# Attention with 16 queries per head: queries transposed on the DVE from eight strided loads, QK weights kept for two chunks, a finer cut of the second last V piece

## The chip, the cores and the metric

The kernel runs on one core of a Trainium2 chip. The metric is the device time of one execution in microseconds (us), the median of several. The record marks every one of them as fast, at a granted clock of 0.894 to 0.926, and each kernel was run beside the kernel before on the same chip.

Words used: PE is the matmul engine and PEld its weight loads, DVE the vector engine, ACT the scalar engine, SP the sync engine, which here does nothing but issue loads. DMA is the set of engines, 16 by the profile's page, that move data between the chip's main memory and the on-chip memory (SBUF). A DMA queue is called by the engine that issues on it. Partitions are the rows of a tile in SBUF: 128 in the 128x2048 of the DVE's lines below.

## The reference

```python
B, H, Sq, Skv, Dh = 8, 16, 16, 2048, 256          # bfloat16 throughout

def reference(q, k, v):
    scale = q.shape[-1] ** -0.5
    scores = jnp.einsum('bhqd,bhkd->bhqk', q, k) * scale
    attn = _softmax(scores, axis=-1)
    return jnp.einsum('bhqk,bhkd->bhqd', attn, v)
```

There are 128 heads. K and V are 134 MB each, q and the output 1 MB each. Every byte of K and V is used for only 16 queries, so the loads were expected to bound the time. In the profile of the kernel before, their queue accounts for 98.5% of the DMA engines.

## The kernel before

It treats eight heads as a group (16 groups) and K and V as 64 pieces of 2 MB each. For K piece `i`, SP loads `KN`; the DVE transposes it into `KB` in two halves, `kt(i,0)` and `kt(i,1)`; PE multiplies it with the query weights `QW` (`qk`). After four pieces the DVE takes the row maximum, ACT does the exponential, the DVE transposes the result (`pt`, `px`), and PE multiplies with V (`pv`). The queries reach `QW` through PE transposes (`qprep`) and a scaling copy on ACT (`qwb`).

```python
NT = 64; PT_TOK = 32; R_KN = 3; R_KB = 4; R_V = 5        # buffers: 3 K pieces, 4 K halves, 5 V pieces
qg = q.rearrange("b h s d -> (b h s) d").rearrange("(g p) d -> p g d", p=128)
# ... the order of the loads on SP: K0, q, K1, K2, K3, K4, V0, K5, V1, ...
        for i in range(NP):
            seq.append(("k", i))
            if i == 0:
                seq.append(("q", 0))
            if 4 <= i < NP - 3:
                seq.append(("v", i - 4))
# ...
        tail = {NP - 2: [32], NP - 1: [16, 8, 8]}        # tokens per load of the last two V pieces
        def k_load(i):                                   # a K buffer is free when kt of its old piece is done
            s = i % R_KN
            return J("sp", "ld", lambda eng: eng.dma_start(
                KN[:, s], ku[i // 2, :, PT_TOK * (i % 2):PT_TOK * (i % 2) + PT_TOK, :]),
                [("kt", i - R_KN, 1) if i >= R_KN else None], dma=(sem_kn[s], 16 * (i // R_KN + 1)))
# ...
                j_q = J("sp", "ld", lambda eng: eng.dma_start(QR[:], qg), dma=(sem_q, 16))
# ...
        def kt(i, h):                                    # a K half waits for the QK that used its buffer
                j_kt[i, h] = J("dve", "kt", lambda eng: emit_kt(eng, i, h),
                               [j_k[i], ("qk", i - R_KB // 2, h) if i >= R_KB // 2 else None])
        def qk(i):                                       # one job of 8 matmuls for each half
                for c in range(2):
                    j_qk[i, c] = J("pe", "qk", lambda eng, c=c: emit_qk(eng, i, c),
                                   [("kt", i, c), ("qwb", g), ("exp", g - 1, i % 2) if g and i % 4 < 2 else None])
# ... the order on the DVE
        kt(0, 0)
        kt(0, 1)
        for g in range(G):
            for r in (1, 2, 3):
                kt(4 * g + r, 0)
                kt(4 * g + r, 1)
            # max(g); kt(4g+4, 0); pt(g), px(g), small sums; kt(4g+4, 1); eviction of group g-1
```

The DVE works through its list in order: while it waits at one operation, the work behind it waits too. In this program SP issues K `i+3` only when `kt(i,1)` is done, and a V load behind a waiting K load waits with it (V0 goes out behind K4, at 21.5 us). And `kt(i+2)` cannot start before `qk(i)` has used the buffer.

Of the kernel before, what the change touches and what calls it, by code (L numbers as in the profile page):

```python
# [4 lines left out]
ACTF = mybir.ActivationFunctionType  # L5
ALU = mybir.AluOpType
AX = mybir.AxisListType
BF16 = mybir.dt.bfloat16
F32 = mybir.dt.float32
# [4 lines left out]
R_KB = 4  # L14
R_V = 5
# [10 lines left out]
def bass_standalone__softmax_full_bidir__sampling_kernel(  # L26
# [6 lines left out]
    B, H, SQ, D = q.shape  # L33
# [3 lines left out]
    G = NH // 8  # L37
    NP = 4 * G
    scale = float(D) ** -0.5
# [1 line left out]

    ku = k.rearrange("b h s d -> (b h s) d").rearrange("(u p t) d -> u p t d", p=128, t=NT)
    vu = v.rearrange("b h s d -> (b h s) d").rearrange("(u p t) d -> u p t d", p=128, t=NT)
    qg = q.rearrange("b h s d -> (b h s) d").rearrange("(g p) d -> p g d", p=128)

    with ExitStack() as es:
        ec = es.enter_context
        KN = ec(nc.sbuf_tensor("KN", [128, R_KN, PT_TOK, D], BF16))
        KB = ec(nc.sbuf_tensor("KB", [128, R_KB, PT_TOK // 2, D], BF16))
        VB = ec(nc.sbuf_tensor("VB", [128, R_V, PT_TOK, D], BF16))  # L50
        QR = ec(nc.sbuf_tensor("QR", [128, G, D], BF16))
        QW = ec(nc.sbuf_tensor("QW", [128, 2, 2, 8, 128], BF16))
        P_sb = ec(nc.sbuf_tensor("P_sb", [128, 2048], BF16))
        PC = ec(nc.sbuf_tensor("PC", [128, 2, NT // 2, 32], BF16))
# [10 lines left out]

        S_ps = ec(nc.psum_tensor("S_ps", [128, 4, 512], F32))
        O_ps = ec(nc.psum_tensor("O_ps", [128, 3, 512], F32))
        XP_ps = ec(nc.psum_tensor("XP_ps", [128, 8, 128], BF16))

        sem_kn = [ec(nc.semaphore("s_kn%d" % i)) for i in range(R_KN)]  # L70
        sem_v = [ec(nc.semaphore("s_v%d" % i)) for i in range(R_V)]
# [17 lines left out]

        block = ec(nc.Block())  # L90

        KNf = KN[:].bitcast(F32)
        KBf = KB[:].bitcast(F32)

        def ap_of(t_ap, offset, dims):
            return bass.AP(tensor=t_ap.tensor, offset=offset, ap=[list(t_ap.ap[0])] + [list(d) for d in dims])
# [8 lines left out]
            iv = ident[:]  # L105
            return eng.tensor_reduce(out=mask[:], in_=ap_of(iv, iv.offset, [[1, 2], [2, 64]]), axis=AX.X, op=ALU.add)

        def emit_qprep(eng, g):
            qv = QR[:, g, :]
            for bp in range(8):  # L110
                b, par = bp // 2, bp % 2
                for a in range(4):
                    ins = eng.transpose(XP_ps[32 * a:32 * a + 32, bp, :], ap_of(qv, qv.offset + 64 * b + par, [[2, 32]]),  # L113
                                        ident[:], tile_position=(0, 32 * a))
            return ins

        def emit_qwb(eng, g):
            for a in range(4):
                dv = QW[32 * a:32 * a + 32, g % 2, 0, 0, :]
                sv = XP_ps[32 * a:32 * a + 32, 0, :]  # L120
                ins = eng.activation(ap_of(dv, dv.offset + 32 * a, [[8 * 128 + 1, 2], [128, 8], [2, 16]]),  # L121
                                     ap_of(sv, sv.offset + 16 * a, [[64, 2], [128, 8], [1, 16]]),
                                     ACTF.Copy, scale=scale)
            return ins

        def emit_kt(eng, i, h):
# [1 line left out]
            return eng.transpose(KBf[:, (2 * i + h) % R_KB].rearrange("p t i -> p (t i)"),  # L128
                                 KNf[:, i % R_KN].rearrange("p t i -> p (t i)")[:, n * h:n * h + n])

        def emit_qk(eng, i, c):
            g, Gh, half = i // 4, (i % 4) // 2, i % 2
            kb0 = KB[:, (2 * i + c) % R_KB, 0, :]
            for bp in range(8):
                b, par = bp // 2, bp % 2
                ins = eng.matmul(S_ps[:, 2 * half + c, :], QW[:, g % 2, Gh, bp, :],  # L136
                                 ap_of(kb0, kb0.offset + 64 * b + par, [[D, 16], [2, 32]]),
                                 start=(Gh == 0 and bp == 0), stop=(Gh == 1 and bp == 7))
            return ins

        def emit_max(eng, g):
            return eng.tensor_reduce(out=negm[:, g:g + 1], in_=S_ps[:].rearrange("p c n -> p (c n)"),  # L142
                                     axis=AX.X, op=ALU.max, negate=True)
# [45 lines left out]
        for j in range(NP):  # L189
            g, r = j // 4, j % 4  # L190
            v_of.append((2 * g + r % 2, r // 2) if g < last - 1 else (2 * g + r // 2, r % 2))
        seq = []
        for i in range(NP):
            seq.append(("k", i))
            if i == 0:
                seq.append(("q", 0))
            if 4 <= i < NP - 3:
                seq.append(("v", i - 4))
            elif i == NP - 2:
                seq.append(("v", i - 5))  # L200
        seq += [("v", j) for j in range(NP - 6, NP)]

        j_k, j_v, j_kt, j_qk, j_pv = {}, {}, {}, {}, {}
        j_qwb, j_qprep, j_exp, j_pt, j_px, j_max, j_rab = {}, {}, {}, {}, {}, {}, {}
        j_ea, j_eb, j_st = {}, {}, {}
        tail = {NP - 2: [32], NP - 1: [16, 8, 8]}

        def k_load(i):
            s = i % R_KN
# [8 lines left out]
        def v_load(j, a, n, sem):  # L218
            u, h = v_of[j]
            if j < NP - 2:  # L220
                deps = [("pvuse", j - R_V)] if j >= R_V else []
            else:
                deps = [("kt", j - 1, 0), ("kt", j - 1, 1)]
            return J("sp", "ld", lambda eng: eng.dma_start(  # L224
                v_buf(j)[:, a:a + n, :], vu[u, :, PT_TOK * h + a:PT_TOK * h + a + n, :]), deps, dma=sem)

        for what, i in seq:
            if what == "k":
                j_k[i] = k_load(i)
            elif what == "q":  # L230
                j_q = J("sp", "ld", lambda eng: eng.dma_start(QR[:], qg), dma=(sem_q, 16))
            elif i < NP - 2:
                j_v[i] = [v_load(i, 0, PT_TOK, (sem_v[i % R_V], 16 * (i // R_V + 1)))]
            else:
                parts, a = [], 0
                for x, n in enumerate(tail[i]):
                    sem = ec(nc.semaphore("s_vt%d_%d" % (i, x)))
                    parts.append(v_load(i, a, n, (sem, 16)))
                    a += n
                j_v[i] = parts  # L240

        def qprep(g):
            if g < G:
                j_qprep[g] = J("pe", "qprep", lambda eng: emit_qprep(eng, g), [j_q, j_ident, ("qwb", g - 1) if g else None])

        def qwb(g):
            if g < G:
                j_qwb[g] = J("act", "qwb", lambda eng: emit_qwb(eng, g),
                             [("qprep", g), j_qwz, ("qk", 4 * g - 5, 1) if g >= 2 else None])

        def kt(i, h):
            if i < NP:
                j_kt[i, h] = J("dve", "kt", lambda eng: emit_kt(eng, i, h),
                               [j_k[i], ("qk", i - R_KB // 2, h) if i >= R_KB // 2 else None])

        def qk(i):
            if i < NP:
                g = i // 4
                for c in range(2):
                    j_qk[i, c] = J("pe", "qk", lambda eng, c=c: emit_qk(eng, i, c),  # L260
                                   [("kt", i, c), ("qwb", g), ("exp", g - 1, i % 2) if g and i % 4 < 2 else None])

        def pv(g, p):
            if g < 0:
# [47 lines left out]
                            dma=(sem_st[g % 2], 16 * (g // 2 + 1)))  # L312


        qprep(0)
        qprep(1)
        for g in range(G):
            if g < last:
                qk(4 * g)
                qk(4 * g + 1)  # L320
                pv(g - 1, 0)
                qk(4 * g + 2)
                qk(4 * g + 3)
                pv(g - 1, 1)
                qprep(g + 2)
            else:
                qk(4 * g)
                qk(4 * g + 1)
                pv_single(4 * g - 4)
                qk(4 * g + 2)  # L330
                pv_single(4 * g - 3)
                qk(4 * g + 3)
                for j in range(4 * g - 2, NP):
                    pv_single(j)
# [10 lines left out]

        kt(0, 0)
        kt(0, 1)
        for g in range(G):
            for r in (1, 2, 3):
                kt(4 * g + r, 0)  # L350
                kt(4 * g + r, 1)
            j_max[g] = J("dve", "max", lambda eng, g=g: emit_max(eng, g), [("qk", 4 * g + 3, 1)])
            kt(4 * g + 4, 0)
            for h in range(2):
                j_pt[g, h] = J("dve", "pt", lambda eng, g=g, h=h: emit_pt(eng, g, h), [("exp", g, h)])
            for h in range(2):
                j_px[g, h] = J("dve", "px", lambda eng, g=g, h=h: emit_px(eng, g, h),
                               [("pt", g, h), j_ptz, pt_free(g - 1, h)])
            js = J("dve", "sm", lambda eng, g=g: eng.tensor_reduce(  # L359
                out=ltot[:, g:g + 1], in_=lsum[:, g, :], axis=AX.X, op=ALU.add), [("exp", g, 0), ("exp", g, 1)])  # L360
            jr = J("dve", "sm", lambda eng, g=g: eng.reciprocal(rinv[:, g:g + 1], ltot[:, g:g + 1]), [js])  # L361
            j_rab[g] = J("dve", "sm", lambda eng, g=g: eng.tensor_scalar(  # L362
                out=rab[:, g, :], in0=mask[:], scalar1=rinv[:, g:g + 1], scalar2=None, op0=ALU.mult), [jr, j_mask])
            kt(4 * g + 4, 1)
            evac_b(g - 1)
        evac_b(last)

        tables = {"kt": j_kt, "qwb": j_qwb, "qprep": j_qprep, "qk": j_qk, "exp": j_exp, "pt": j_pt, "px": j_px, "max": j_max,
                  "rab": j_rab, "ea": j_ea, "eb": j_eb, "st": j_st, "pv": j_pv}

        def resolve(d):
# [71 lines left out]
```

## Time and profile before

| | before |
|---|---|
| time, median | 646.72 us |
| span in the profile | 644.9 us |
| K, V and q packets | from 1.7 to 639.4 us of the span |
| DMA rate from 100 to 600 us | 428 GB/s |

The first view is the page's strip of 40 equal slices of the span: the busy share of the DMA engines in tenths, and what they moved. The second is the page's table of queues (packets, MB, share of 16 engines); q1 is SP's queue, q10 ACT's.

```profile
DMA  9999999999999999999999999999999999999995
GB/s 341 425 430 426 429 426 430 424 432 426 428 427 428 429 428 428 428 426 429 428 426 431 426 428 428 430 426 427 429 428 427 430 426 429 426 429 429 429 426 209
...
q1 hardware_dynamic: 19248, 269.49, 98.5%
q10 hardware_dynamic: 2304, 1.05, 0.6%
```

DMA is at 9 everywhere but at the very end, and the K/V queue alone accounts for 98.5% of the engines. The loads are the bound. The next line is from SP's own waits (who waited for whom, us in total, times, longest):

```profile
SPq L210 <- DVE KB L128: 525.2, 61, 16.5
```

SP waits 525 us for K buffers, and this costs nothing: a load lands 24 to 28 us after its issue (median 23.6 for K, 27.8 for V), though 2 MB at 428 GB/s take only 4.9 us (2.1 / 0.428), so four to five loads are always queued. A change can move the time only where this queue is empty or the rate falls. These are the start and the end. Here is the start on the DVE, from the timeline (start, duration, engine, line, operation, count, and in brackets the idle time before it and what ended it):

```profile
8.14 4.50 DVE L128 STREAM_TRANSPOSE KB<-KN 128x2048 f32<-128x2048 f32 x2 [5.00 <-DMA KN<-in_k_dram]
16.61 4.50 DVE L128 STREAM_TRANSPOSE KB<-KN 128x2048 f32<-128x2048 f32 x2 [3.97 <-DMA KN<-in_k_dram]
21.51 4.51 DVE L128 STREAM_TRANSPOSE KB<-KN 128x2048 f32<-128x2048 f32 x2 [0.39 <-DMA KN<-in_k_dram]
```

K0 lands at 8.1 us and the DVE follows each K piece as it lands. SP's part of the same stretch, from the same view:

```profile
0.73 0.37 SPq L210 DMA_DIRECT2D KN<-in_k_dram  x1
1.32 0.84 SPq L231 DMA_DIRECT2D QR<-in_q_dram  x1
21.51 0.43 SPq L224 DMA_DIRECT2D VB<-in_v_dram  x1
```

q goes out behind K0 in one load; V0 follows K4 at 21.5 us, when kt(1) is done. And this is the end, on PE:

```profile
625.04 3.65 PE L171 MATMUL O_ps<-VB,PT 128*128 128x256 bf16 x32 [0.76 <-DMA VB<-in_v_dram]
629.94 3.65 PE L171 MATMUL O_ps<-VB,PT 128*128 128x256 bf16 x32 [1.24 <-DMA VB<-in_v_dram]
634.84 7.16 PE L171 MATMUL O_ps<-KN,PT 128*128 128x256 bf16 x64 [1.25 <-DMA KN<-in_v_dram]
```

PE waits three times for V (0.76, 1.24 and 1.25 us). The last 64 matmuls, of the second last and the last piece, start when the second last piece, one load of 32 tokens, has landed.

### The profile page before, as it was taken

To read this page: it belongs to the slowest core of one execution; us is meant where nothing else is said; L and a number is where in the kernel's file an instruction comes from. 1 tells how busy PE (TensorE), PEld (TensorE's weight loads), DVE (VectorE), ACT (ScalarE), POOL (GpSimd) and SP (SyncE) were. 2 spreads that over 40 slices of the span, in tenths; PEclk is the share of its full clock that TensorE was granted. 3 is DMA by queue.
4 is the path that set the end of the run, shared out by engine and by line. 5 is a ranking of instruction groups with operands and counts; after the bars stand their busy time and mean duration, and the time that the engine had idled before them with its cause. 6 is when DMAs were issued, how large, how long until landed. Compare 5 with 4: busy or idle time off the path is not lost.

```text
span 644.9 us, 6273 instructions
## 1 busy us (share of the span) xinstructions
PE 515.9 (80%) x2688; PEld 226.4 (35%) x2688; DVE 427.2 (66%) x370; ACT 74.1 (11%) x145; POOL 4.2 (1%) x7
## 2 busy tenths in 40 slices
PE   1849887778987779876798787797878797787996
PEld 1314333333333334332343233333323342333575
DVE  3886865857667585765948749477485854957760
ACT  2020200102011020110202002020020200201010
POOL 2000000000000000000000000000000000000000
PEclk9978988898888899887989788988879987899999
DMA  9999999999999999999999999999999999999995
GB/s 341 425 430 426 429 426 430 424 432 426 428 427 428 429 428 428 428 426 429 428 426 431 426 428 428 430 426 427 429 428 427 430 426 429 426 429 429 429 426 209
DMA packets 21580, 270.94 MB, mean 420 GB/s; under 512 B 2352, under 2 KB 4400, under 8 KB 5168
## 3 DMA queue, kind: packets, MB, share of 16 engines
q1 hardware_dynamic: 19248, 269.49, 98.5%
q10 hardware_dynamic: 2304, 1.05, 0.6%
q8 instruction: 21, 0.34, 0.2%
q14 instruction: 7, 0.06, 0.0%
HBM read 269.48 MB, written 1.05 MB: 419 GB/s over the span
## 4 chain that ended last, share of the span: by engine, by line
DMA 46%; DVE 33%; PE 16%; issue 4%; SPq 0%
DMA KN<-in_k_dram 42%; DVE KB L128 17%; PE S_ps L136 14%; DVE PT L157 7%; DVE negm L142 5%; DMA KN<-in_v_dram 4%; DVE PC L151 3%; PE O_ps L171 2%; PE O_ps L165 1%; DVE rinv L361 0%; DVE ltot L359 0%; DVE O_fin L305 0%; DVE rab L362 0%; SPq L224 0%
## 5 line engine op out<-in xcount | busy, mean ns | idle before, releaser
L128 DVE STREAM_TRANSPOSE KB<-KN 128x2048 f32<-128x2048 f32 x128 | 289.4, 2291 | 143.2 <-DMA KN<-in_k_dram 143.2
L136 PE MATMUL S_ps<-KB,QW 128*128 128x512 bf16 x1024 | 287.9, 441 | 109.2 <-DVE KB L128 109.2
L136 PEld LDWEIGHTS S_ps<-KB,QW 128*128 128x128 bf16 x1024 | 106.1, 108 | 282.1 <-DVE KB L128 129.7
L165 PE MATMUL O_ps<-VB,PT 128*128 128x512 bf16 x896 | 197.9, 379 | 0.0
L165 PEld LDWEIGHTS O_ps<-VB,PT 128*128 128x128 bf16 x896 | 87.5, 98 | 105.9
L146 ACT ACTIVATE P_sb<-S_ps,negm 128x1024 bf16<-128x1024 f32 x32 | 35.3, 1109 | 495.8 <-DVE negm L142 495.8
L142 DVE TENSOR_REDUCE negm<-S_ps 128x1 f32<-128x2048 f32 x16 | 36.7, 2292 | 51.9 <-PE S_ps L136 51.9
L157 DVE COPY PT<-PC 32x1024 bf16<-32x1024 bf16 x128 | 52.9, 413 | 1.8
L151 DVE STREAM_TRANSPOSE PC<-P_sb 128x1024 bf16<-128x1024 bf16 x32 | 37.3, 1204 | 1.3 <-ACT P_sb L146 1.3
L121 ACT ACTIVATE QW<-XP_ps 32x256 bf16<-32x256 bf16 x64 | 28.6, 446 | 47.3 <-PE XP_ps L113 46.8
L171 PE MATMUL O_ps<-VB,PT 128*128 128x256 bf16 x192 | 21.8, 272 | 2.0 <-DMA VB<-in_v_dram 2.0
L113 PE MATMUL XP_ps<-ident,QR 128*32 128x128 bf16 x512 | 10.9, 232 | 13.6 <-DMA QR<-in_q_dram 11.7
L171 PEld LDWEIGHTS O_ps<-VB,PT 128*128 128x128 bf16 x192 | 18.6, 98 | 5.3 <-issue 1.5
L305 DVE SCALAR_TENSOR_TENSOR O_fin<-O_ps,rab,O_tmp 128x256 bf16<-128x256 f32 x16 | 7.2, 447 | 14.3 <-PE O_ps L171 14.1
L113 PEld LDWEIGHTS XP_ps<-ident,QR 128*32 128x32 bf16 x512 | 7.9, 102 | 19.8 <-DMA QR<-in_q_dram 11.7
L297 ACT ACTIVATE O_tmp<-O_ps,rab 128x256 f32<-128x256 f32 x16 | 7.6, 473 | 13.8 <-PE O_ps L171 11.2
L171 PE MATMUL O_ps<-KN,PT 128*128 128x256 bf16 x64 | 7.2, 273 | 1.3 <-DMA KN<-in_v_dram 1.3
L171 PEld LDWEIGHTS O_ps<-KN,PT 128*128 128x128 bf16 x64 | 6.2, 98 | 2.2 <-DMA KN<-in_v_dram 1.5
L146 ACT ACTIVATION_READ_ACCUMULATOR P_sb<-S_ps,negm 128x1 f32 x32 | 6.3, 196 | 0.0
L362 DVE TENSOR_SCALAR rab<-mask,rinv 128x2 f32<-128x2 f32 x16 | 3.7, 228 | 0.6
L182 POOL MEMSET PT<- 128x4096 f32 x1 | 3.5, 3511 | 0.0
L361 DVE RECIPROCAL rinv<-ltot 128x1 f32<-128x1 f32 x16 | 2.6, 164 | 0.6
(10 smaller groups left out, 6.6 us busy)
## 6 DMA issues: line engine op xcount, KB each, us to landing
KN<-in_k_dram SPq DMA_DIRECT2D x64, 2048.0 KB, 23.6
VB<-in_v_dram SPq DMA_DIRECT2D x62, 2048.0 KB, 27.8
KN<-in_v_dram SPq DMA_DIRECT2D x1, 2048.0 KB, 27.6
out_dram<-O_fin ACTq DMA_DIRECT2D x16, 64.0 KB, 9.4
KN<-in_v_dram SPq DMA_DIRECT2D x1, 1024.0 KB, 29.6
KN<-in_v_dram SPq DMA_DIRECT2D x2, 512.0 KB, 30.7
QR<-in_q_dram SPq DMA_DIRECT2D x1, 0.5 KB, 10.4
```

The source lines that it names most:

```text
L113: ins = eng.transpose(XP_ps[32 * a:32 * a + 32, bp, :], ap_of(qv, qv.offset + 64 * b + par, [[2, 32]]), ident[:], tile_position=(0, 32 * a))
L121: ins = eng.activation(ap_of(dv, dv.offset + 32 * a, [[8 * 128 + 1, 2], [128, 8], [2, 16]]), ap_of(sv, sv.offset + 16 * a, [[64, 2], [128, ...
L128: return eng.transpose(KBf[:, (2 * i + h) % R_KB].rearrange("p t i -> p (t i)"), KNf[:, i % R_KN].rearrange("p t i -> p (t i)")[:, n * h:n ...
L136: ins = eng.matmul(S_ps[:, 2 * half + c, :], QW[:, g % 2, Gh, bp, :], ap_of(kb0, kb0.offset + 64 * b + par, [[D, 16], [2, 32]]), start=(Gh ...
L142: return eng.tensor_reduce(out=negm[:, g:g + 1], in_=S_ps[:].rearrange("p c n -> p (c n)"), axis=AX.X, op=ALU.max, negate=True)
L146: return eng.activation(P_sb[:, 1024 * h:1024 * h + 1024], S_ps[:, 2 * h:2 * h + 2, :].rearrange("p c n -> p (c n)"), ACTF.Exp, bias=negm[ ...
L151: return eng.transpose(PC[:, h].rearrange("p t x -> p (t x)"), P_sb[:, 1024 * h:1024 * h + 1024])
L157: ins = eng.tensor_copy(PT[pr, 32 * h:32 * h + 32, pr], PC[pr, h])
L165: ins = eng.matmul(O_ps[:, g % 2, :], PT[:, t, :], rhs, start=(t == 0), stop=(t == NT - 1))
L171: ins = eng.matmul(O_ps[:, bank, D * Gh:D * Gh + D], PT[:, t, :], buf[:, t - base, :], start=(t == 0), stop=(t == NT - 1))
L297: j_ea[g] = J("act", "ea", lambda eng: eng.activation(O_tmp[:], O_ps[:, g % 2, 0:D], ACTF.Copy, scale=rab[:, g, 0:1]), [dep, ("rab", g), ( ...
L305: j_eb[g] = J("dve", "eb", lambda eng: eng.scalar_tensor_tensor(out=O_fin[:, g % 2, :], in0=O_ps[:, bank, D:2 * D], scalar=rab[:, g, 1:2], ...
```

## The change

The intent: get rid of the 512 small PE transposes of the queries by letting the DVE transpose all queries at once; load each QK weight once for two K halves; and let PE start on the second last V piece when half of it has landed. For the single DVE operation the program lays the queries in the partitions in another order, so q is loaded by eight strided loads (16 partitions each, every second partition of 32), and these were put on ACT's queue. They use the space of the fifth V buffer until it is needed. The core of the diff (cuts marked with `...`):

```diff
-    qg = q.rearrange("b h s d -> (b h s) d").rearrange("(g p) d -> p g d", p=128)
+    qx = q.rearrange("b h s d -> (b h s) d").rearrange("(g e a s) d -> e a s g d", e=2, a=4, s=16)
 ...
-        def emit_qprep(eng, g):
-            ...                                   # 32 PE transposes into PSUM per group
+        def emit_qload(eng, e, a):
+            qv = QR[32 * a + e:32 * a + 32:2, :, :]
+            return eng.dma_start(qv, qx[e, a])
+
+        def emit_qt(eng):
+            return eng.transpose(QT[:].bitcast(F32).rearrange("p g d -> p (g d)"),
+                                 QR.bitcast(F32).rearrange("p g d -> p (g d)"))
 ...
+        def mm_kept(eng, out_ap, lhs, rhs, start, stop):      # matmul with ldweights=False
+            ...
-        def emit_qk(eng, i, c):
+        def emit_qk(eng, i):
             for bp in range(8):
-                ...                               # one matmul
+                for c in range(2):                # the second one keeps the weights
+                    ...
 ...
+        j_q = [J("act", "ldq", lambda eng, e=e, a=a: emit_qload(eng, e, a), dma=(sem_q, 128))
+               for e in range(2) for a in range(4)]
             seq.append(("k", i))
-            if i == 0:
-                seq.append(("q", 0))
 ...
-        tail = {NP - 2: [32], NP - 1: [16, 8, 8]}
+        tail = {NP - 2: [16, 16], NP - 1: [16, 8, 8]}
 ...
-                               [j_k[i], ("qk", i - R_KB // 2, h) if i >= R_KB // 2 else None])
+                               [j_k[i], ("qk", i - R_KB // 2) if i >= R_KB // 2 else None])
 ...
-                for c in range(2):
-                    j_qk[i, c] = J("pe", "qk", ..., [("kt", i, c), ("qwb", g), ...])
+                j_qk[i] = J("pe", "qk", ..., [("kt", i, 0), ("kt", i, 1), ("qwb", g), ...])
 ...
         kt(0, 0)
         kt(0, 1)
+        j_qt[0] = J("dve", "qt", emit_qt, j_q)
         for g in range(G):
```

More of the change, by code (lines that the diff above doesn't have):

```diff
@@ L50, in bass_standalone__softmax_full_bidir__sampling_kernel @@
         VB = ec(nc.sbuf_tensor("VB", [128, R_V, PT_TOK, D], BF16))
-        QR = ec(nc.sbuf_tensor("QR", [128, G, D], BF16))
+        QT = ec(nc.sbuf_tensor("QT", [128, G, D], BF16))
         QW = ec(nc.sbuf_tensor("QW", [128, 2, 2, 8, 128], BF16))
@@ L67, in bass_standalone__softmax_full_bidir__sampling_kernel @@
         O_ps = ec(nc.psum_tensor("O_ps", [128, 3, 512], F32))
-        XP_ps = ec(nc.psum_tensor("XP_ps", [128, 8, 128], BF16))
         sem_kn = [ec(nc.semaphore("s_kn%d" % i)) for i in range(R_KN)]
@@ L90, in bass_standalone__softmax_full_bidir__sampling_kernel @@
         block = ec(nc.Block())
+        QR = VB[:, R_V - 1, 0:G, :]
         KNf = KN[:].bitcast(F32)
@@ L106, in emit_mask @@
             return eng.tensor_reduce(out=mask[:], in_=ap_of(iv, iv.offset, [[1, 2], [2, 64]]), axis=AX.X, op=ALU.add)
-        def emit_qprep(eng, g):
-            qv = QR[:, g, :]
-            for bp in range(8):
-                b, par = bp // 2, bp % 2
-                for a in range(4):
-                    ins = eng.transpose(XP_ps[32 * a:32 * a + 32, bp, :], ap_of(qv, qv.offset + 64 * b + par, [[2, 32]]),
-                                        ident[:], tile_position=(0, 32 * a))
-            return ins
+        def emit_qload(eng, e, a):
[4 more added lines that the diff above has]
+                                 QR.bitcast(F32).rearrange("p g d -> p (g d)"))
         def emit_qwb(eng, g):
             for a in range(4):
-                dv = QW[32 * a:32 * a + 32, g % 2, 0, 0, :]
-                sv = XP_ps[32 * a:32 * a + 32, 0, :]
-                ins = eng.activation(ap_of(dv, dv.offset + 32 * a, [[8 * 128 + 1, 2], [128, 8], [2, 16]]),
-                                     ap_of(sv, sv.offset + 16 * a, [[64, 2], [128, 8], [1, 16]]),
-                                     ACTF.Copy, scale=scale)
+                for e in range(2):
+                    pr = slice(32 * a, 32 * a + 32)
+                    dv, sv = QW[pr, g % 2, e, 0, :], QT[pr, g, :]
+                    ins = eng.activation(ap_of(dv, dv.offset + 32 * a + e, [[256, 4], [128, 2], [2, 16]]),
+                                         ap_of(sv, sv.offset + 2 * e, [[64, 4], [1, 2], [4, 16]]),
+                                         ACTF.Copy, scale=scale)
             return ins
@@ L129, in emit_kt @@
                                  KNf[:, i % R_KN].rearrange("p t i -> p (t i)")[:, n * h:n * h + n])
-        def emit_qk(eng, i, c):
+        def mm_kept(eng, out_ap, lhs, rhs, start, stop):
+            return eng.add_instruction(mybir.InstMatmult(
+                start_tensor_calc=start, stop_tensor_calc=stop, ldweights=False, tile_size=(128, 128),
+                tile_position=(0, 0), name=nc.get_next_instruction_name(), engine=eng.engine,
+                ins=[eng.lower_ap(rhs), eng.lower_ap(lhs, for_matmul_weights=True)], outs=[eng.lower_ap(out_ap)]))
+        def emit_qk(eng, i):
             g, Gh, half = i // 4, (i % 4) // 2, i % 2
-            kb0 = KB[:, (2 * i + c) % R_KB, 0, :]
             for bp in range(8):
                 b, par = bp // 2, bp % 2
-                ins = eng.matmul(S_ps[:, 2 * half + c, :], QW[:, g % 2, Gh, bp, :],
-                                 ap_of(kb0, kb0.offset + 64 * b + par, [[D, 16], [2, 32]]),
-                                 start=(Gh == 0 and bp == 0), stop=(Gh == 1 and bp == 7))
+                for c in range(2):
+                    kb0 = KB[:, (2 * i + c) % R_KB, 0, :]
+                    rhs = ap_of(kb0, kb0.offset + 64 * b + par, [[D, 16], [2, 32]])
+                    mm = eng.matmul if c == 0 else (lambda *x, **y: mm_kept(eng, *x, **y))
+                    ins = mm(S_ps[:, 2 * half + c, :], QW[:, g % 2, Gh, bp, :], rhs,
+                             start=(Gh == 0 and bp == 0), stop=(Gh == 1 and bp == 7))
             return ins
@@ L203, in bass_standalone__softmax_full_bidir__sampling_kernel @@
         j_k, j_v, j_kt, j_qk, j_pv = {}, {}, {}, {}, {}
-        j_qwb, j_qprep, j_exp, j_pt, j_px, j_max, j_rab = {}, {}, {}, {}, {}, {}, {}
+        j_qwb, j_qt, j_exp, j_pt, j_px, j_max, j_rab = {}, {}, {}, {}, {}, {}, {}
         j_ea, j_eb, j_st = {}, {}, {}
-        tail = {NP - 2: [32], NP - 1: [16, 8, 8]}
+        tail = {NP - 2: [16, 16], NP - 1: [16, 8, 8]}
         def k_load(i):
@@ L220, in v_load @@
             if j < NP - 2:
-                deps = [("pvuse", j - R_V)] if j >= R_V else []
+                deps = [("pvuse", j - R_V)] if j >= R_V else [("qt", 0)] if j == R_V - 1 else []
             else:
@@ L229, in bass_standalone__softmax_full_bidir__sampling_kernel @@
                 j_k[i] = k_load(i)
-            elif what == "q":
-                j_q = J("sp", "ld", lambda eng: eng.dma_start(QR[:], qg), dma=(sem_q, 16))
             elif i < NP - 2:
@@ L240, in bass_standalone__softmax_full_bidir__sampling_kernel @@
                 j_v[i] = parts
-        def qprep(g):
-            if g < G:
-                j_qprep[g] = J("pe", "qprep", lambda eng: emit_qprep(eng, g), [j_q, j_ident, ("qwb", g - 1) if g else None])
         def qwb(g):
@@ L248, in qwb @@
                 j_qwb[g] = J("act", "qwb", lambda eng: emit_qwb(eng, g),
-                             [("qprep", g), j_qwz, ("qk", 4 * g - 5, 1) if g >= 2 else None])
+                             [("qt", 0), j_qwz, ("qk", 4 * g - 5) if g >= 2 else None])
         def kt(i, h):
@@ L258, in qk @@
                 g = i // 4
-                for c in range(2):
-                    j_qk[i, c] = J("pe", "qk", lambda eng, c=c: emit_qk(eng, i, c),
-                                   [("kt", i, c), ("qwb", g), ("exp", g - 1, i % 2) if g and i % 4 < 2 else None])
+                j_qk[i] = J("pe", "qk", lambda eng: emit_qk(eng, i),
+                            [("kt", i, 0), ("kt", i, 1), ("qwb", g), ("exp", g - 1, i % 2) if g and i % 4 < 2 else None])
         def pv(g, p):
@@ L312, in store @@
                             dma=(sem_st[g % 2], 16 * (g // 2 + 1)))
-        qprep(0)
-        qprep(1)
         for g in range(G):
@@ L324, in bass_standalone__softmax_full_bidir__sampling_kernel @@
                 pv(g - 1, 1)
-                qprep(g + 2)
             else:
@@ L351, in bass_standalone__softmax_full_bidir__sampling_kernel @@
                 kt(4 * g + r, 1)
-            j_max[g] = J("dve", "max", lambda eng, g=g: emit_max(eng, g), [("qk", 4 * g + 3, 1)])
+            j_max[g] = J("dve", "max", lambda eng, g=g: emit_max(eng, g), [("qk", 4 * g + 3)])
             kt(4 * g + 4, 0)
@@ L366, in bass_standalone__softmax_full_bidir__sampling_kernel @@
         evac_b(last)
-        tables = {"kt": j_kt, "qwb": j_qwb, "qprep": j_qprep, "qk": j_qk, "exp": j_exp, "pt": j_pt, "px": j_px, "max": j_max,
+        tables = {"kt": j_kt, "qwb": j_qwb, "qt": j_qt, "qk": j_qk, "exp": j_exp, "pt": j_pt, "px": j_px, "max": j_max,
                   "rab": j_rab, "ea": j_ea, "eb": j_eb, "st": j_st, "pv": j_pv}
```

## The prediction

> **What bounds the kernel now.** The loads. The page's 40-slice strip shows DMA at 9 in every slice but the last, 424 to 434 GB/s from slice 2; the queue table gives 98.5% of 16 engines to the K/V queue. The sync engine waits 525 us in total for the DVE's K transposes (its waits), yet a load lands 24 to 28 us after issue against about 4.9 us of transfer, so four or five loads are always queued. Time can change only where DMA runs dry: before about 1.7 us (first packet), at the start, and after the last packet (639.4 us of a 644.9 us span; timed runs say 646.7).
>
> **Removed.** 512 PE transposes (10.9 us busy) and 512 of 1024 QK weight loads (53 of 226 us PEld). Warm QK matmuls already come every 0.21 us with loads under them: worth nothing in the middle. QK now needs both K halves, and a K buffer frees after 16 matmuls instead of 8: later, but a group's DVE chain is about 36 us by my sum (DVE busy 427/16 = 27 plus waits), against 39 us of DMA.
>
> **Tail, gained.** In the last timeline PE finishes the previous V piece at 633.6, waits until 634.84 for a 32-token piece, then runs 64 matmuls (7.16 us) to 642.0. Split 16+16, the first half should land near 632.4, so PE goes on at 633.6 and ends near 641.0, held a little by the last landing (639.9). Gain about 1.0 us.
>
> **Start, lost.** Before, q followed K0 on the same queue: K0 landed at 8.1, q at 11.7. Now q comes as eight loads on ACT's queue beside K0, K1, K2. [...] a store's eight 512-byte packets per engine take 5.0 to 6.8 us between 16 KB packets of 0.61 us, and 0.35 us alone at the end. q was 32 packets of 2 KB per engine (plus now eight semaphore writes); each should wait for one K packet. K0 to K3 are 32 K packets per engine, so I estimate q to land with K3, near 25 to 26 us, not 11.7. The DVE queue is in order: kt(0), then the query transpose, then kt(1). K3 needs only kt(0), but K4 and V0 need kt(1). Estimate: q 25.6, query transpose 2.3 -> 28, kt(1) 4.5 -> 32.5, K4's first packet about 33.5. DMA idles from 25 to 33.5 plus 0.6 of ramp: about 9 us. Packets of q between large ones may cost about 0.9 us less than the 3.8 us they took alone. A second gap is near: K7 waits for kt(4,1), about 61 us, with queued loads ending near 63.6.
>
> **Sum.** 646.7 + 9.1 - 0.9 - 1.0 = about 654 us, 1.1% slower. Range 645.4 to 659.0. Faster by over 2%: 0.01; within: 0.94; slower: 0.05.
>
> **Right if** the profile shows q landing past 20 us, the DVE waiting for it with K1 already there, DMA near zero for some 8 us between 25 and 34, one burst of 426+ GB/s afterwards, and PE without its 1.2 us gap before the last piece. PEld falls by about 53 us without effect.
>
> **Wrong if** q lands early (queues served by bytes, or q's packets running ahead): then no gap, about 645 us. If q's packets are 512 bytes each, q lands later, 28 to 30 us, and the loss is 11 to 13 us. A second gap at K7 adds 1 to 3 us. If K buffers freeing later matters, dips appear in every group.

The sum is 646.7 + 9.1 - 0.9 - 1.0 = 653.9 us. That a q packet waits for a K packet stands on the store quoted there. The 9.1 is the 8.5 us from 25 to 33.5 us and 0.6 of ramp, which is what the kernel before lost from 2 to 4 us: 303 GB/s against 428, so 2 x (1 - 303/428) = 0.58 us. For the 0.9, an estimate, the text gives no source; near it is what the kernel before lost from 8 to 12 us, in which q moved: 338 GB/s, so 0.84 us. "Warm": in the trace of the changed kernel QK matmuls come 0.43 us apart from 33 to 38 us, after PE had stood still, and 0.22 us apart from 39 to 41 us.

## The result, and the profile after

| | before | after |
|---|---|---|
| time, median | 646.73 us (4 runs, 646.72 to 646.86) | 658.25 us (4 runs, 657.83 to 658.66) |
| ratio | | 1.0178, 95% interval 1.016 to 1.0195 |
| span in the profile | 644.9 us | 656.0 us |
| last K/V packet | 639.4 us | 650.1 us |
| q landed | 11.7 us | 28.05 us |
| first packet of K4 | queue never empty | 35.8 us |

A ratio here and below is the mean time of one kernel's runs over that of the other's runs of the same rounds, so it is not quite the ratio of the medians quoted. The packet and landing times are read from the packet and landing records of the trace.

The changed kernel is 11.5 us slower. The strip and the queue table of the page after:

```profile
DMA  9689999999999999999999999999999999999995
GB/s 361 215 339 429 412 429 427 427 431 429 423 433 427 432 423 431 430 427 427 429 429 427 430 427 430 426 429 427 428 428 429 428 430 428 427 430 427 430 422 213
...
q1 hardware_dynamic: 18864, 268.44, 96.5%
q10 hardware_dynamic: 4480, 2.10, 1.3%
```

The second, third and fifth slices (16.4 us each) have lost bandwidth: 215, 339 and 412 GB/s where 425, 430 and 429 stood. From the sixth on nothing is lost against before. ACT's queue has 2176 more packets: q now travels in pieces of 512 bytes (2048 packets, the rest are semaphore writes), where the old load had 512 packets of 2 KB.

The DVE at the start:

```profile
8.23 4.50 DVE L129 STREAM_TRANSPOSE KB<-KN 128x2048 f32<-128x2048 f32 x2 [5.09 <-DMA KN<-in_k_dram]
28.08 2.31 DVE L114 STREAM_TRANSPOSE QT<-VB 128x2048 f32<-128x2048 f32 x1 [15.34 <-DMA VB<-in_q_dram]
30.31 4.46 DVE L129 STREAM_TRANSPOSE KB<-KN 128x2048 f32<-128x2048 f32 x2
```

The DVE finishes kt(0) at 12.7 us and then stands for 15.3 us at the query transpose, whose q has not landed, with K1 (landed at 13.6 us) ready behind it. kt(1) ends at 34.8 us instead of 21.1. SP, in the same view, issues K4 and V0 only then (the first row holds the issues of K0 to K4, and K4 is its end):

```profile
0.74 34.39 SPq L220 DMA_DIRECT2D KN<-in_k_dram  x5
35.17 0.43 SPq L234 DMA_DIRECT2D VB<-in_v_dram  x1
```

To see what this did to the loads, here are stretches of the span: the stretch, its length, busy time (and number) of PE, PEld, DVE, ACT and POOL, then granted clock, DMA share and, last, GB/s. First before, then after.

```profile
0.00:10.00 10.00, 0.00 (x0) 0.00 (x0) 3.77 (x3) 1.28 (x1) 4.15 (x7) 1.00 0.83 292
10.00:20.00 10.00, 6.36 (x77) 3.16 (x78) 6.03 (x4) 3.55 (x8) 0.00 (x0) 1.00 1.03 419
20.00:30.00 10.00, 7.98 (x37) 3.21 (x35) 7.89 (x5) 0.00 (x0) 0.00 (x0) 1.00 1.02 431
30.00:40.00 10.00, 5.57 (x53) 2.37 (x54) 7.99 (x6) 3.40 (x7) 0.00 (x0) 0.98 1.00 428
60.00:70.00 10.00, 10.00 (x48) 4.41 (x47) 5.01 (x3) 0.00 (x0) 0.00 (x0) 1.00 1.00 424
100.00:600.00 500.00, 406.90 (x1988) 167.88 (x1987) 339.43 (x297) 57.52 (x113) 0.00 (x0) 0.89 1.01 428
```

```profile
0.00:10.00 10.00, 0.00 (x0) 0.00 (x0) 3.68 (x3) 0.00 (x0) 4.16 (x7) 1.00 0.84 323
10.00:20.00 10.00, 0.00 (x0) 0.00 (x0) 2.74 (x2) 0.00 (x0) 0.00 (x0) 1.00 1.02 405
20.00:30.00 10.00, 0.00 (x0) 0.00 (x0) 1.92 (x1) 1.28 (x1) 0.00 (x0) 1.00 0.76 216
30.00:40.00 10.00, 7.21 (x21) 1.39 (x11) 5.51 (x4) 4.40 (x16) 0.00 (x0) 1.00 0.43 159
60.00:70.00 10.00, 5.09 (x15) 1.02 (x8) 9.06 (x11) 0.00 (x0) 0.00 (x0) 0.55 0.99 393
100.00:600.00 500.00, 395.59 (x1653) 123.95 (x1238) 337.26 (x286) 60.08 (x159) 0.00 (x0) 0.89 1.01 428
```

Time lost against the 428 GB/s of the middle is the length of a stretch times (1 - rate/428). In the five stretches that both fences show, up to 70 us, it is 3.4 us before and 15.0 us after; in the 500 us from 100 us on, the two kernels move data at the same 428 GB/s. The dip from 60 to 70 us (393 GB/s, 0.8 us) is a second, short gap: K7 went out at 64.9 us, when kt(4,1) was done.

The tail on PE:

```profile
638.95 7.16 PE L181 MATMUL O_ps<-VB,PT 128*128 128x256 bf16 x64 [0.64 <-DVE PT L167]
645.94 7.15 PE L181 MATMUL O_ps<-KN,PT 128*128 128x256 bf16 x64
```

The wait for the second last V piece is gone, as meant, but PE is no earlier against the loads: its last matmul ended 2.6 us after the last K/V packet before (642.0 and 639.4), and 3.0 us after it now (653.1 and 650.1). PE has no wait for V left at all. It is now PE, not the landing, that the end waits for.

### The profile page after: what moved, and what is told of

Read it like the earlier page. It is cut to its first block, busy times and chain, and to the rows that moved or that the text cites. A ratio compares the mean times of both kernels' runs of the same rounds, so it can differ in the third digit from the quotient of the medians. Undisturbed runs are those within 1.5% of the kernel's fastest.

```text
span 656.0 us, 4795 instructions
## 1 busy us (share of the span) xinstructions
PE 488.9 (75%) x2176; PEld 166.0 (25%) x1664; DVE 428.9 (65%) x371; ACT 79.2 (12%) x209; POOL 4.2 (1%) x7
## 4 chain that ended last, share of the span: by engine, by line
DVE 38%; DMA 33%; PE 22%; issue 4%; ACTq 3%; ACT 0%; DVEq 0%
DMA KN<-in_k_dram 32%; DVE KB L129 20%; PE S_ps L147 9%; PE S_ps L134 8%; DVE PT L167 7%; DVE negm L152 6%; DVE PC L161 4%; PE O_ps L181 3%; ACTq L111 3%; PE O_ps L175 2%; DMA VB<-in_q_dram 1%; DVE rinv L362 0%; DVE ltot L360 0%; DVE QT L114 0%; ACT QW L122 0%
## 5 line engine op out<-in xcount | busy, mean ns | idle before, releaser
L147 PE MATMUL S_ps<-KB,QW 128*128 128x512 bf16 x512 | 218.4, 427 | 163.6 <-DVE KB L129 130.7
L134 PE MATMUL S_ps<-KB,QW 128*128 128x512 bf16 x512 | 216.1, 422 | 0.0
L147 PEld LDWEIGHTS S_ps<-KB,QW 128*128 128x128 bf16 x512 | 53.9, 105 | 369.4 <-DVE KB L129 184.4
L122 ACT ACTIVATE QW<-QT 32x128 bf16<-32x128 bf16 x128 | 35.0, 334 | 7.9 <-DVE QT L114 7.3
L308 DVE SCALAR_TENSOR_TENSOR O_fin<-O_ps,rab,O_tmp 128x256 bf16<-128x256 f32 x16 | 7.2, 447 | 11.5 <-PE O_ps L181 11.5
L114 DVE STREAM_TRANSPOSE QT<-VB 128x2048 f32<-128x2048 f32 x1 | 2.3, 2312 | 15.3 <-DMA VB<-in_q_dram 15.3
L122 ACT ACT_TABLE_LOAD x1 | 1.3, 1283 | 21.9 <-issue 21.9
```

Of the source, the lines that this page charges most:

```text
L122: ins = eng.activation(ap_of(dv, dv.offset + 32 * a + e, [[256, 4], [128, 2], [2, 16]]), ap_of(sv, sv.offset + 2 * e, [[64, 4], [1, 2], [4 ...
L134: return eng.add_instruction(mybir.InstMatmult(start_tensor_calc=start, stop_tensor_calc=stop, ldweights=False, tile_size=(128, 128), tile ...
L147: ins = mm(S_ps[:, 2 * half + c, :], QW[:, g % 2, Gh, bp, :], rhs, start=(Gh == 0 and bp == 0), stop=(Gh == 1 and bp == 7))
```

## The experiments

The twelve runs are told with what was expected of each before it ran.

**Theories.** (S) Starvation: the small q packets on a queue of their own take turns with the big K packets, q lands when K has run dry, the DVE's order keeps kt(1) behind q, and DMA stands idle until K4. Rival (A): the paired QK frees the K buffers too late, all through the run. Rival (B): 2048 small packets are dear in themselves. Rival (D): q's lateness matters only because the DVE's list has it in front of kt(1).

### Query loads back on SP's queue, behind K0

```diff
         for i in range(NP):
             seq.append(("k", i))
+            if i == 0:
+                seq.append(("q", 0))
 ...
-        j_q = [J("act", "ldq", ...) for e in range(2) for a in range(4)]      # at the start, on ACT
+            elif what == "q":
+                j_q = [J("sp", "ldq", ...) for e in range(2) for a in range(4)]
```

> The changed kernel with one edit: the eight query loads go out on the sync engine's queue behind K0, where the old kernel had its one load, not on ACT's queue. Starvation theory (the query packets took turns with 16 KB K packets, so q landed at 28 us, and K4 and V0 were issued too late): q now lands at about 12 to 13 us, no stretch without DMA near 27 to 36 us, no second dip near 66 us, and the time falls by about 10 us to 646 to 648 us. Rival A (pairing the QK matmuls frees the K buffers too late and costs all through the run): stays near 657 to 658 us. Rival B (the 2048 packets of 512 B are dear in themselves): falls only by the little that their place matters, to 655 us or so.

Measured: 648.46 us (4 runs, 647.42 to 648.85), 1.0022 of before. q landed at 13.3 us, and the strip of its page has no gap, only the slow drain of q in the first slice:

```profile
GB/s 300 430 426 428 427 427 428 428 427 429 429 426 429 429 425 430 428 426 429 429 426 428 427 429 426 428 428 429 427 427 429 427 429 426 429 428 427 430 421 220
```

One edit, where the loads are queued, gives back 9.8 of the 11.5 us. Rival A and rival B fall as the main cause. The time is 0.5 us above what S expected (646 to 648), so something of 1.5 us is left for the next runs.

### Query transpose after kt(1)

```diff
-        j_qt[0] = J("dve", "qt", emit_qt, j_q)
         for g in range(G):
             for r in (1, 2, 3):
                 kt(4 * g + r, 0)
                 kt(4 * g + r, 1)
+                if g == 0 and r == 1:
+                    j_qt[0] = J("dve", "qt", emit_qt, j_q)
```

> The changed kernel with one edit: on the DVE the query transpose comes after kt(1,0) and kt(1,1), so K4 and V0 are issued without waiting for q. Theory of the DVE's order (q's late landing hurts only because it stands in the DVE queue ahead of kt(1)): the first gap closes, 647 to 650 us. Starvation theory with turns packet by packet: q cannot land until the K and V traffic runs dry, and two more loads are now in front of it; q lands at 36 to 37 us, kt(2) waits for QK(0), hence for q, K5's first packet comes near 52 us, and DMA is dry for about 16 us, not 9: 664 to 667 us, slower than the changed kernel.

Measured: 668.77 us (4 runs), 1.034 of before, slower than the changed kernel by 10.5 us. The DVE:

```profile
13.77 4.50 DVE L129 STREAM_TRANSPOSE KB<-KN 128x2048 f32<-128x2048 f32 x2 [0.93 <-DMA KN<-in_k_dram]
38.52 2.31 DVE L114 STREAM_TRANSPOSE QT<-VB 128x2048 f32<-128x2048 f32 x1 [20.25 <-DMA VB<-in_q_dram]
```

kt(1) now runs at once, K4 and V0 go out at 18.7 us, and q lands at 38.5 us instead of 28.1, because two more loads stand beside it in the turns. The K and V packets stop at 34.8 us and start again at 54.7 us. Rival D falls: getting the big loads out earlier delayed the small one that everything needs. I had expected a dry time of 16 us and 664 to 667 us; it was 20 us dry, and 668.8.

### One query load on ACT's queue, in the kernel before

```diff
-                j_q = J("sp", "ld", lambda eng: eng.dma_start(QR[:], qg), dma=(sem_q, 16))   # behind K0
+        j_q = J("act", "ldq", lambda eng: eng.dma_start(QR[:], qg), dma=(sem_q, 16))         # at the start
```

> The kernel before with one edit: its single query load goes out on ACT's queue at the start, not on the sync engine's behind K0. Turns packet by packet, with this load's 32 packets of 2 KB per engine, one for each 16 KB packet of K: q lands at 24 to 27 us, not 11.7; kt(1) does not wait for it here but kt(2) waits for QK(0); K5's first packet comes near 37 us, DMA has a gap of 2 to 3 us near 34 to 37 us, and the time is 647.5 to 649.5 us. If ACT's queue itself makes 512-byte packets (rival to: the strided shape makes them), q lands at 36 us or later and the time is over 655 us. If the queues share by bytes or q runs ahead: q lands by 12 us, 645.5 to 646.7 us.

Measured: 653.51 us (4 runs), 1.0099 of before. This load keeps its 2 KB packets on ACT's queue too (401 of them in the table below), so it is not the queue that makes packets small. Its last packet ended at 25.9 us; in the prediction I had put the same number of packets at 25 to 26 us. The turns can be counted in the packet records:

```
                                  16 KB packets   q packets    rate of K, V    rate of q
one load on ACT, 8 to 25 us            371        401 of 2 KB     358 GB/s      48 GB/s
changed kernel, 8 to 22 us             336        351 of 512 B    393 GB/s      13 GB/s
```

In both runs about one q packet went for each large one, at 2 KB (401 to 371) as at 512 bytes (351 to 336). Here kt(1) is not held up by q, yet kt(2) waits for QK(0), which needs q, and DMA is dry from 35.8 to 40.2 us with a second dip at 61 us. I had expected a gap of 2 to 3 us and 647.5 to 649.5 us; it was 4.5 us and 653.5, since I had put QK(0) too early: PE's first QK matmuls came 0.43 us apart (31.0 to 34.8 us), the later ones 0.22. The kernel before had not been safe from this: its own load, moved to another queue, costs 6.6 us.

### K1 held back until q has landed

The changed kernel, its q loads still on ACT's queue:

```diff
-                [("kt", i - R_KN, 1) if i >= R_KN else None], dma=...)
+                [("kt", i - R_KN, 1) if i >= R_KN else None] + (j_q if i == 1 else []), dma=...)
```

> The changed kernel, its eight query loads still on ACT's queue, with one edit: K1 is issued only when q has landed. Starvation theory: only K0 is there to take turns with; once K0 is through, q drains alone at about 225 GB/s and lands near 13 us; K1's first packet comes near 14 us, so DMA loses about 2 us there, and nothing later: 649.5 to 651.5 us, about 8 us faster than the changed kernel although a load was held back. If ACT's queue as such is slow, or the loss lies elsewhere: 656 us or more.

Measured: 649.84 us (4 runs, 648.53 to 650.04), 1.0042 of before. q's last packet ended at 12.2 us, K1's first came at 13.8 us, and the time lies in the 649.5 to 651.5 us expected. An added wait takes 8.4 us off. ACT's queue as such is not slow: from 8 to 11 us q moved on it at 226 GB/s, and on SP's queue in the first experiment at 231. What hurts is other traffic in the turns.

### What the tail and the pairing are worth alone

The kernel before with one line changed:

```diff
-        tail = {NP - 2: [32], NP - 1: [16, 8, 8]}
+        tail = {NP - 2: [16, 16], NP - 1: [16, 8, 8]}
```

> The kernel before with one edit: the second last V piece is loaded as 16+16 tokens, not 32. My reading of the tail: the last DMA packet stays at 639.4 us of the span, PE no longer waits 1.25 us before the last 64 matmuls, PE ends near 641.0, and the time falls by about 1.0 us to 645.7 us. Rival (PE is not what ends the tail, or the finer loads land no earlier): no change.

Measured: 645.99 us (5 runs, 645.79 to 646.14) beside 646.93 of before, ratio 0.9986 (0.9973 to 0.9998). PE in the tail:

```profile
630.08 3.65 PE L171 MATMUL O_ps<-VB,PT 128*128 128x256 bf16 x32 [0.90 <-DMA VB<-in_v_dram]
633.57 3.66 PE L171 MATMUL O_ps<-KN,PT 128*128 128x256 bf16 x32
637.61 3.67 PE L171 MATMUL O_ps<-KN,PT 128*128 128x256 bf16 x32 [0.38 <-DMA KN<-in_v_dram]
```

PE goes on at 633.57 us without its 1.25 us of waiting. My reading of the tail held: 0.94 us for an expected 1.0.

The kernel before with the paired QK alone, as in the change:

```diff
-                               [j_k[i], ("qk", i - R_KB // 2, h) if i >= R_KB // 2 else None])
+                               [j_k[i], ("qk", i - R_KB // 2) if i >= R_KB // 2 else None])
-                for c in range(2):
-                    j_qk[i, c] = J("pe", "qk", ..., [("kt", i, c), ...])
+                j_qk[i] = J("pe", "qk", ..., [("kt", i, 0), ("kt", i, 1), ...])      # second matmul of each pair: weights kept
```

> The kernel before with one edit: the QK matmuls of the two K halves alternate with the weights kept, as one job that needs both halves and frees both. Mine: the middle is bound by DMA, the queue never runs dry, weight loads fall by about 53 us of busy time without effect; the softmax of the last group comes about 1.7 us later and is absorbed by PE's 3.3 us of waits in the tail: within 0.5 us of 646.7. Rival A (this pairing is the main loss): several us slower, with dips in every group.

Measured: 646.76 us (5 runs, 646.55 to 647.34), ratio 1.0001. The 512 weight loads saved are worth nothing in the time, and in the changed kernel, which pairs too, the rate in the middle is the same 428 GB/s. But the maximum of the last group and PE's tail show where the pairing does act; first before, then the pairing alone:

```profile
617.33 2.29 DVE L142 TENSOR_REDUCE negm<-S_ps 128x1 f32<-128x2048 f32 x1 [2.60 <-PE S_ps L136]
```

```profile
619.91 2.29 DVE L151 TENSOR_REDUCE negm<-S_ps 128x1 f32<-128x2048 f32 x1 [5.33 <-PE S_ps L133]
627.49 7.16 PE L180 MATMUL O_ps<-VB,PT 128*128 128x256 bf16 x64 [0.64 <-DVE PT L166]
634.67 7.16 PE L180 MATMUL O_ps<-KN,PT 128*128 128x256 bf16 x64
```

The maximum comes 2.6 us later (I had said 1.7). In the kernel before, PE does the first half of a group's first K piece while the DVE is busy with the softmax transposes (8 matmuls at 590.3 us); the paired job needs both halves, and kt(60,1) comes after those transposes. PE's waits for V in the tail (3.3 us together) swallow the delay, and PE then runs 128 matmuls without a pause from 627.5 to 641.8 us.

Both together, in the kernel before (the two diffs above added up):

> The kernel before with both the paired QK and the 16+16 split of the second last V piece, nothing of the queries. The tail split alone took 0.94 us off, pairing alone changed nothing but used up PE's wait in the tail (the last max came 2.6 us later). If the split works only through that wait: no gain here, within 0.3 us of 646.8. If the two are independent: 645.9.

Measured: 646.33 us median, but the five runs fall in two heaps (646.17, 646.30, 646.33 and 647.59, 647.76); ratio 1.0000 (0.9987 to 1.0014). The profiled run, one of the 646.3 heap, ended PE at 641.6 us, 0.2 us before the pairing alone. The median lies 0.5 us under the 646.8 of the first expectation, outside its 0.3 us; the mean (646.8) agrees with it. So on the mean no gain of the split is seen beside the pairing. That the wait it was to remove is already used up fits the tail shown above, but the two heaps keep these runs from showing it. Why there are two heaps is open, as only one run of each kernel has a profile.

### The changed kernel with q on SP and the old QK

The edit of the first experiment, and the pairing undone:

```diff
-                j_qk[i] = J("pe", "qk", ..., [("kt", i, 0), ("kt", i, 1), ...])
+                for c in range(2):
+                    j_qk[i, c] = J("pe", "qk", ..., [("kt", i, c), ...])
-                               [j_k[i], ("qk", i - R_KB // 2) if i >= R_KB // 2 else None])
+                               [j_k[i], ("qk", i - R_KB // 2, h) if i >= R_KB // 2 else None])
```

> The changed kernel with the query loads on the sync engine's queue behind K0 and with the QK matmuls of the old kernel (each half its own job, weights loaded for each). If the strided query loads, once in their place, cost only their slower drain (5 us of DMA for 1 MB, not 3.8), and unpairing gives the tail its wait back for the 16+16 split to use: 646.4 to 647.4 us, about 1 us under the run that kept the pairing (648.5). If pairing has no part in that run's 1.5 us: 648.5 again.

Measured: 647.06 us (5 runs, 646.90 to 647.21), ratio 1.0002. That is 1.4 us under the run that kept the pairing. Its PE waits in the tail again (0.63 and 0.64 us). The 1.07 us that it lies above the tail split alone (645.99) match its last K/V packet, 1.04 us later (640.64 and 639.60): q's slower drain.

Of the 1.4 us the profiles show a part only. The profiled run with the pairing was the fastest of its four (647.42 us), 0.36 us above the profiled run here: its last K/V packet came 0.6 us sooner (640.02 us), but PE ended 2.7 us after that packet, and here 1.7. So 1.0 us is seen in the tail; the slower runs of the paired kernel (648.10 to 648.85 us) have no profile, and what they lost is not shown.

### Why q drained slowly

Once it is alone, q of the changed kernel moves at 219 GB/s (1472 packets from 23.9 to 27.3 us), half the normal rate. Is it the small packets, or the small loads? Three other cuts of the query load were tried in the kernel before, on SP's queue behind K0. First eight loads of 16 neighbouring partitions:

```diff
-                j_q = J("sp", "ld", lambda eng: eng.dma_start(QR[:], qg), dma=(sem_q, 16))
+                j_q = [J("sp", "ld", lambda eng, x=x: eng.dma_start(QR[16 * x:16 * x + 16], qg[16 * x:16 * x + 16]),
+                         dma=(sem_q, 128)) for x in range(8)]
```

> The kernel before with one edit: its query load is cut into eight loads of 16 neighbouring partitions each, on the same queue in the same place. It asks what made the packets 512 bytes: if the step of two partitions did, the packets stay 2 KB, q drains in about 3.8 us and the time stays at 646.9 us; if the number of partitions in a load did, the packets are 512 bytes, q drains in about 5 us and the time is about 1 us longer.

Measured: 652.18 us (4 runs), ratio 1.0082. The packets were 512 bytes, so it is not the step that makes them small but the smaller loads (16 partitions and 128 KB each; which of the two counts is not separated). But q drained in 8.6 us, not 5, and the loss was 5.2 us, not 1. The step of the changed kernel had been a help. Then the same with every eighth partition:

```diff
-                j_q = [... eng.dma_start(QR[16 * x:16 * x + 16], qg[16 * x:16 * x + 16]) ... for x in range(8)]
+                j_q = [... eng.dma_start(QR[x:128:8], qg[x:128:8]) ... for x in range(8)]
```

> The kernel before with its query load cut into eight loads of 16 partitions each on the same queue, as in the run with neighbouring partitions (652.2 us, q drained in 8.6 us at 118 GB/s), but each load takes every eighth partition, so it spans all 128. Packets again 512 bytes. If the span of partitions sets the drain (16 neighbours 118 GB/s, 32 partitions 225): 290 GB/s or more here, q drained in 3.7 us or less, 646.5 to 647.2 us. If the number of partitions or the packet size sets it: 8 us again, 652 us.

Measured: 649.23 us (4 runs), ratio 1.0036. Neither expectation was met: about 210 GB/s, between the two. The span of the partitions alone does not set the drain: these loads span all 128 and moved no faster than those of every second of 32 (207 and 236 GB/s below). The last cut was four loads of every fourth partition:

```diff
-                j_q = [... eng.dma_start(QR[x:128:8], qg[x:128:8]), dma=(sem_q, 128)) for x in range(8)]
+                j_q = [... eng.dma_start(QR[x:128:4], qg[x:128:4]), dma=(sem_q, 64)) for x in range(4)]
```

> The kernel before with its query load cut into four loads of 32 partitions each, every fourth partition, on the same queue. The three cuts measured so far drained at 118 GB/s (16 neighbouring partitions), 225 (every second of 32) and about 215 (every eighth of 128). [...] 290 GB/s or more, q drained in 3.8 us or less as in the old single load, 646.5 to 647.3 us. If small packets set it (512 bytes here too): 215 to 225 GB/s, 5 to 5.6 us, 648 to 649.5 us.

Measured: 646.91 us (4 runs), ratio 1.0000, with the same 512-byte packets; the time and the rate (318 GB/s below) are those of the first outcome. One stretch, 8 to 10 us, while q alone is moving (last column GB/s), of: sixteen neighbours, every second of 32 (the run with q on SP), every eighth, every fourth, and the old single load:

```profile
8.00:10.00 2.00, 0.00 (x0) 0.00 (x0) 1.32 (x1) 0.00 (x0) 0.00 (x0) 1.00 1.27 118
```

```profile
8.00:10.00 2.00, 0.00 (x0) 0.00 (x0) 1.56 (x1) 0.00 (x0) 0.00 (x0) 1.00 1.23 236
```

```profile
8.00:10.00 2.00, 0.00 (x0) 0.00 (x0) 1.70 (x1) 0.00 (x0) 0.00 (x0) 1.00 1.06 207
```

```profile
8.00:10.00 2.00, 0.00 (x0) 0.00 (x0) 1.86 (x1) 0.00 (x0) 0.00 (x0) 1.00 1.18 318
```

```profile
8.00:10.00 2.00, 0.00 (x0) 0.00 (x0) 1.86 (x1) 0.00 (x0) 0.00 (x0) 1.00 1.07 301
```

118, 236, 207, 318 and 301 GB/s, in this order. The size of the packets does not set the drain: with 512 bytes in the fourth of these runs q moved no slower than with 2 KB in the last, 318 and 301 GB/s, both under the 428 GB/s of the K loads. In the first three the loads are alike in number and size (eight of 16 partitions), and with the choice of partitions the rate went from 118 to 207 and 236 GB/s; between the first and the third (118 and 207) nothing else was changed. The fourth also changed the loads from eight of 16 partitions to four of 32, so there the choice of partitions is not the only change. What it is in the choice of partitions that sets the rate was not shown.

### A tail cut finer still

The kernel before with a finer cut of the last piece too:

```diff
-        tail = {NP - 2: [32], NP - 1: [16, 8, 8]}
+        tail = {NP - 2: [16, 16], NP - 1: [8, 8, 8, 8]}
```

> The kernel before with the tail split a step further: 16+16 tokens and then 8+8+8+8, not 16+8+8. In the run with 16+16 alone PE still waited 0.38 us before the last 32 matmuls and ended 1.2 us after the last landing. Expected to take that wait away: 645.7 us, 0.3 us under that run's 646.0, if the smaller loads land on time; the same 646.0 if they do not.

Measured: 645.83 us (5 runs, 645.77 to 645.89), ratio 0.9984 (0.9972 to 0.9997). It is the fastest kernel measured, 1 us under the kernel before; against the 16+16 split alone, 0.16 us, which runs of two different calls do not settle.

## Why the prediction was right or wrong

The measured 658.25 us lies in the range and in the class "within 2%", with the mechanism as predicted. The predicted 654.0 was 4.3 us too low.

- **Right: DMA bounds the time, and only start and end count.** From 100 to 600 us both kernels move 428 GB/s. Saving 512 weight loads changed nothing (the pairing alone: 1.0001). The PE transposes have no run of their own; the kernel that drops them but keeps the old QK and the old queue is not faster than before (1.0002).
- **Right: turns packet by packet.** 351 q packets to 336 K packets in 14 us are those turns. q landed past 20 us, the DVE stood with K1 ready, and DMA was dry.
- **Wrong: "q was 32 packets of 2 KB per engine", carried over from the old load to the new ones.** They made 128 packets of 512 bytes per engine. With 2 KB packets q is through at 25.9 us (the run with one load on ACT); with 512 bytes only 576 of 2048 packets were through when K3 was (23.9 us), about one for each of the 512 packets of K0 to K3, and the remaining 1472 had to drain afterwards, at 219 GB/s, in 3.4 us. So q landed at 28.05 and not 25.6 us, and K4's first packet came at 35.8 and not 33.5 us. The prediction had named 512-byte packets as a way to be wrong, with 28 to 30 us and a loss of 11 to 13 us, and that is what came.
- **Mis-sized: "9.1 - 0.9" for the start.** The packet records give, against 428 GB/s, 3.7 us lost in the first 40 us before and 14.5 after: 10.8 us for a predicted 8.2. Up to 20 us the changed kernel lost 0.3 us less than the old one (3.3 and 3.6), so interleaving saved a third of the 0.9; from 20 to 40 us it lost 11.2 us more, where the prediction had 9.1: K4 came 2.3 us later than predicted.
- **Mis-sized: the second gap near K7.** It was seen coming, with K7 at about 61 us and queued loads to 63.6, and counted as nothing. It was K7 at 64.9 us and 0.8 us lost, since everything was later.
- **Wrong: the tail's gain "about 1.0 us".** The reading was right for the split alone (0.94 us). Beside the pairing no gain is seen: PE ended 2.97 us after the last packet, not 2.64, so 0.3 us were lost. The step that failed is the sentence that pairing is hidden ("39 us of DMA" against 36): it held for the middle, but in the tail the pairing makes the last softmax 2.6 us later and uses up the wait that the split was to free.

The sum in the profiles: 10.8 + 0.8 + 0.3 = 11.9 us, less some 0.6 us by which the changed kernel lost less than the old one between 40 and 60 us and in the long rest, is 11.3; the span of the changed kernel is 11.1 us longer, so 0.2 us stay unassigned. The times give the total another way: 9.8 us (the queue) + 1.4 (pairing, where the split is there too) + 1.07 (drain) - 0.94 (split alone) = 11.3 of the measured 11.5. The term of 1.4 rests on two kernels run in different calls, of which the one with pairing spread by 1.4 us; its cause in the tail is shown for the kernel before, and here the two profiles show 1.0 us of it.

What is left open: the two heaps of times of the kernel with paired QK and the split, the like spread of the changed kernel with q on SP (647.42 to 648.85 us), why a load of 16 or 32 partitions is made into 512-byte packets and one of 128 partitions into 2 KB, and why the choice of partitions changes the rate at which q drains.

## What to carry to other kernels

In a kernel bound by its loads, look at a small load that something early depends on: put it in the queue of the big loads at the place where it is needed, for on a queue of its own it got, in these runs, one packet per big packet (351 to 336, 401 to 371) and landed when the big loads ran dry, and sending the big loads sooner only made it later (38.5 us for 28.1). Ask of every wait that a change removes whether another part of the same change has already used it up. And when a load is cut up, measure more than one choice of partitions for its parts: in the kernel before it was 646.9 us with four loads of every fourth partition, 649.2 with eight of every eighth, and 652.2 with eight of 16 neighbours.

## What the issues on ACT's queue took

SP was spared an issue of 0.84 us, but on ACT's queue five of the eight issues took 0.63 to 0.72 us each and the next two 7.36 and 9.42 us, as the chain of waits of the changed kernel shows (start, us, what). ACT's activation table was loaded only after them, at 21.9 us and not at 3.1. That cost nothing here, as q landed later still (28.05 us). Why these two issues took so long was not shown.

```profile
3.64 0.63 ACTq L111
4.30 7.36 ACTq L111
11.68 9.42 ACTq L111
```
